# The QKV half-runs of units 1 to 3 moved ahead of the 320-column half-runs of the second product

## The chip, the cores and the metric

The kernel runs on one core of one Trainium2 chip. The metric is the device time of one execution in microseconds (us). Three runs of the kernel before gave 1107.3, 1107.57 and 1108.79 us, with a median of 1107.57 us.

Five engines work side by side and are tied together by semaphores: TensorE (PE in the profile, with its weight loads shown apart as PEld), VectorE (DVE), ScalarE (ACT), GpSimd (POOL), and SyncE (SP), which issues most DMAs. Products are written to PSUM and copied from there to SBUF by ACT or DVE.

## The reference, cut to what matters

```python
xn = _layernorm(x)                                   # 2048 x 576
qkv = xn @ wqkv                                      # 576 x 1728; 32 heads of 18
idx = pos[:, None] - 2 * arange(8)[None, :]          # window 8, dilation 2
logits = where(idx >= 0, (q . k[idx]) * 18 ** -0.5, -1e9)
o = softmax(logits) . v[idx]                         # per head
h = maximum(xn @ w1, 0)                              # 576 x 4608
return x + o @ wo + h @ w2                           # 4608 x 576
```

## The kernel before, in words

**Phases and token blocks.** A window with dilation 2 joins only tokens of one parity, so the kernel runs two phases (`ph` 0 and 1), the even and the odd 1024 tokens. A phase has four token blocks (`tb`) of 256. Products are float32 split into a high and a low part, and the PE array is used as two halves of 64 rows, so matmuls come in pairs.

**Groups and steps.** After some plain products (the slots) the MLP of a phase runs in 30 groups `g` of eight steps each (`group`, `step`). A step has first a block of the first product (w1), six pairs of 256 columns into a PSUM bank of the pools `ph` and `pm`; I call it an **R block**. Then it has one half of a run of the second product (w2), `o_half`, six pairs into a buffer of the pool `po`. A run of the second product is a piece: 256 or 320 columns of the output, two halves. The 320-column pieces have their halves at steps 2 and 3 and at steps 6 and 7, the 256-column pieces at steps 4 and 5 and at steps 8 and 1 of the next group. I call these halves **O320** and **O256**. A finished piece is copied out by ACT (`evict`, L746) and added to the output by a POOL-issued DMA (L752).

**QKV.** The heads are split into four units of eight heads. Unit 0 belongs to the slots and is not touched. Units 1, 2 and 3 start at groups 5, 11 and 17 of each phase. For each token block, `qkv_half` runs a first half of 14 pairs and a second half of 13 pairs of 432 columns (L142 in `mm_rows`), into one buffer of `po`; after the second half ACT copies the result to the attention arena `att` (L533): four copies in an odd unit, where V has rows of its own, two in an even unit. In the units touched, one token block takes half a group, so a unit lasts two groups.

**Pools.** `po` has two buffers of two banks, `pm` and `ph` two each, so that PSUM is full. Second-product pieces and QKV blocks take the two `po` buffers in turn; whoever takes a buffer waits until its last user was copied out.

**Attention.** It runs on DVE, a few operations at a time, from a list `bg` that `run_bg` works off twice per step as far as a count of DVE time against PE time allows (`STEP`, `DUE`, `room`). Per unit the order is: eight multiplications q by k (L575) and eight sums (L578), the last of which is followed by a POOL select for the mask (L581), then the softmax: maximum (L587), subtraction (L590), exponential on ACT (L593), sum (L596), reciprocal (L599), multiplication (L602), then the weighted sum of v (L610, L617) and transposes (L626, L633), and DMAs of the result to the DRAM tile `od` (L639). A unit's attention lasts until the next unit's QKV or beyond: the softmax of unit `u - 1` stands near the first QKV block of unit `u` (that of unit 0 near the first of unit 1).

**What sets the order.** All engines take their instructions in the order in which the program issues them. In `step` that order is: R block, its copies (seeds L1026, kept banks L1030), the eviction of a 256-column piece at even steps, loads and splits that are due (`fire`, weight splits L172, L174, L176), the first `run_bg`, the O half, the eviction of a 320-column piece at odd steps, late copies, `fire` again, then the QKV half that the table `ins` holds for this step (L1272), then the second `run_bg`.

**After unit 3.** With its attention done the output product's weights are loaded (L267, L270) and split (L172 and L176, 576 columns wide), and at the seam between the phases the second phase's transposed tokens `xT` are loaded (L405, L407).

## Time and profile before

| | |
|---|---|
| runs | 1107.3, 1107.57, 1108.79 us; median 1107.57 |
| profiled execution, span | 1106.7 us |
| granted PE clock (slices and windows) | 0.9 or more in each slice; 1.00 in the QKV stretch 164.32 to 209.20 us |
| matmuls and weight loads | 16410 each |
| DVE, ACT, POOL busy | 843.0, 572.3, 358.3 us |
| HBM | 154 GB/s over the span |

The profiled execution's own time is not listed apart from its span; the runs lie 0.6 to 2.1 us above the span, the median 0.9 us above it. A run of the kernel before differs from another by 0.1% (1107.3 against 1108.79).

How to read it: the timeline gives the start and the duration of each instruction, with equal instructions that follow one another merged. Ends of matmuls are modelled, so the pace of PE is read from one start to the next and not from the durations. A row's bracket says how long its engine stood idle before it and which instruction released it. `64*128 64x432` is a matmul with 64 rows of the array, 128 columns of weights and 432 columns of data.

### The profile page before, as it was taken

To read this page: it belongs to the slowest core of one execution; us is meant where nothing else is said; L and a number is where in the kernel's file an instruction comes from. 1 tells how busy PE (TensorE), PEld (TensorE's weight loads), DVE (VectorE), ACT (ScalarE), POOL (GpSimd) and SP (SyncE) were. 2 spreads that over 40 slices of the span, in tenths; PEclk is the share of its full clock that TensorE was granted. 3 is DMA by queue.
4 is the path that set the end of the run, shared out by engine and by line. 5 is a ranking of instruction groups with operands and counts; after the bars stand their busy time and mean duration, and the time that the engine had idled before them with its cause. 6 is when DMAs were issued, how large, how long until landed. Compare 5 with 4: busy or idle time off the path is not lost.

```text
span 1106.7 us, 37929 instructions
## 1 busy us (share of the span) xinstructions
PE 1098.4 (99%) x16410; PEld 1086.7 (98%) x16410; DVE 843.0 (76%) x1262; ACT 572.3 (52%) x1350; POOL 358.3 (32%) x377
## 2 busy tenths in 40 slices
PE   8999999999999999999999999999999999999998
PEld 8999999999999999999999999999999999999998
DVE  7676898898898989994426339987988978989741
ACT  5433563564465366656535246535635644665551
POOL 2313441333333234432211224413423333343321
PEclk9999999999999999999999999999999999999999
DMA  7369995696597598889958258849947965988896
GB/s 236 133 172 218 201 180 98 147 203 108 118 226 133 84 215 159 157 152 251 276 91 174 28 131 166 151 71 191 201 86 157 195 119 117 216 144 168 156 231 144
DMA packets 136598, 177.26 MB, mean 160 GB/s; under 512 B 27872, under 2 KB 83936, under 8 KB 136400
## 3 DMA queue, kind: packets, MB, share of 16 engines
q0 software_dynamic: 37632, 81.40, 47.3%
q1 hardware_dynamic: 98080, 92.55, 28.7%
q8 instruction: 129, 2.11, 0.7%
q10 hardware_dynamic: 720, 0.89, 0.2%
q14 instruction: 37, 0.30, 0.1%
HBM read 74.07 MB, written 96.22 MB: 154 GB/s over the span
## 4 chain that ended last, share of the span: by engine, by line
PE 96%; DMA 1%; DVE 1%; ACT 1%; issue 0%; DVEq 0%; POOL 0%; ACTq 0%
PE po L163 33%; PE po L142 22%; PE ph L163 16%; PE pm L163 13%; PE pm L142 5%; PE ph L142 4%; PE ph L130 1%; PE po L130 1%; DMA xT<-words 1%; PE pm L354 0%; DMA att<-in_x 0%; DVE ar L176 0%; DVE ar L797 0%; ACT ev L746 0%; ACT ar L172 0%
## 5 line engine op out<-in xcount | busy, mean ns | idle before, releaser
L163 PE MATMUL po<-ar 64*128 64x320 f32 (+1 forms) x5760 | 453.1, 290 | 0.6
L163 PEld LDWEIGHTS po<-ar 64*128 64x128 f32 x5760 | 394.6, 185 | 2.8 <-ACT ev L746 0.8
L163 PE MATMUL ph<-xT,ar 64*128 64x256 f32 x2520 | 317.5, 275 | 0.4 <-ACT pm L1026 0.4
L752 POOL DMA_DIRECT2D out<-ev x128 | 152.5, 1191 | 475.8 <-ACT ev L746 359.1
L163 PEld LDWEIGHTS ph<-xT,ar 64*128 64x128 f32 x2520 | 285.4, 185 | 1.4 <-ACT pm L1026 1.2
L163 PE MATMUL pm<-xS,ar 64*128 64x256 f32 x2160 | 257.5, 275 | 0.7 <-ACT u L1030 0.2
L746 ACT ACTIVATE ev<-po 128x512 f32<-128x512 f32 (+1 forms) x266 | 172.1, 652 | 137.0 <-PE po L163 78.8
L163 PEld LDWEIGHTS pm<-xS,ar 64*128 64x128 f32 x2160 | 235.8, 185 | 1.8 <-ACT u L1030 1.0
L176 DVE TENSOR_TENSOR ar<-st,ar 128x256 fp32r<-128x256 f32 (+3 forms) x236 | 141.3, 619 | 72.7 <-ACT ar L172 72.3
L172 ACT ACTIVATE ar<-st 128x256 fp32r<-128x256 f32 (+3 forms) x304 | 146.0, 503 | 3.3 <-DMA st<-in_w 2.3
L142 PE MATMUL po<-wq,xT 64*128 64x432 f32 x1296 | 133.4, 353 | 0.0
L142 PEld LDWEIGHTS po<-wq,xT 64*128 64x128 f32 x1296 | 119.2, 185 | 3.0 <-ACT ev L746 0.2
L174 POOL TENSOR_TENSOR ar<-st,ar 128x256 fp32r<-128x256 f32 (+1 forms) x68 | 75.0, 1105 | 130.9 <-ACT ar L172 128.1
L958 POOL TENSOR_TENSOR st<-st 128x256 f32<-128x256 f32 x120 | 112.8, 945 | 6.0 <-DMA st<-in_w 1.8
L163 PE MATMUL ph<-xS,ar 64*128 64x256 f32 x720 | 102.0, 275 | 0.0
L163 PEld LDWEIGHTS ph<-xS,ar 64*128 64x128 f32 x720 | 94.3, 185 | 0.2
L575 DVE TENSOR_TENSOR pr<-att 128x1152 f32<-128x1152 f32 x64 | 90.8, 1431 | 0.1
L610 DVE TENSOR_TENSOR pr<-att 128x1152 f32<-128x1152 f32 x64 | 88.4, 1397 | 0.4
L578 DVE TENSOR_REDUCE att<-pr 128x64 f32<-128x1152 f32 x64 | 85.5, 1343 | 0.1
L617 DVE TENSOR_TENSOR pr<-pr 128x1152 f32<-128x1152 f32 x64 | 71.6, 1119 | 1.4
L142 PE MATMUL po<-ar 64*128 64x256 f32 (+1 forms) x984 | 72.5, 290 | 0.0
L797 DVE SCALAR_TENSOR_TENSOR ar<-ph,ar 128x256 fp32r<-128x256 f32 x96 | 39.1, 418 | 42.3 <-ACT ar L793 41.9
(120 smaller groups left out, 1370.6 us busy)
## 6 DMA issues: line engine op xcount, KB each, us to landing
out<-ev POOLq DMA_DIRECT2D x128, 576.0 KB, 7.1
st<-in_w SPq DMA_DIRECT2D x72, 288.0 KB, 5.6
st<-in_w SPq DMA_DIRECT2D x63, 256.0 KB, 3.4
att<-att SPq DMA_DIRECT2D x16, 441.0 KB, 4.4
att<-in_wqkv SPq DMA_DIRECT2D x28, 216.0 KB, 6.2
od<-att SPq DMA_DIRECT2D x32, 160.0 KB, 5.9
att<-in_x SPq DMA_DIRECT2D x14, 288.0 KB, 4.0
st<-in_w SPq DMA_DIRECT2D x60, 64.0 KB, 6.1
```

The costliest lines, as they stand in the source:

```text
L142: ins = nc.tensor.matmul(o, l[z], r[z], start=start, stop=stop)
L163: b.ins = nc.tensor.matmul(b.ap, l[part], r[part], start=start, stop=stop, skip_group_check=skip)
L172: nc.scalar.activation(hi, src, AF.Copy)
L174: nc.gpsimd.tensor_tensor(lo, src, f32(hi), op=ALU.subtract)
L176: nc.vector.tensor_tensor(lo, src, f32(hi), op=ALU.subtract)
L575: nc.vector.tensor_tensor(pr[i], q, window(k, i), op=ALU.mult)
L578: nc.vector.tensor_reduce(lg[:, i], pr.pop(i).rearrange(heads, d=Dh), axis=AX.X, op=ALU.add)
L610: nc.vector.tensor_tensor(pr[i].rearrange(heads, d=Dh), e, window(v, i).rearrange(heads, d=Dh), op=ALU.mult)
L617: nc.vector.tensor_tensor(o, z[:, :, 0:n], z[:, :, n : 2 * n], op=ALU.add)
L746: nc.scalar.activation(acc[:, :, cols], z[:, :, 0 : cols.stop - cols.start], AF.Copy)
L752: ADDED[ph, tb] = nc.gpsimd.dma_start(rows_of(ph, tb), acc, accum_op=ALU.add)
L958: nc.gpsimd.tensor_tensor(stg(o), stg(a), stg(b), op=op)
```

## The change

The half-runs of one QKV block stand one step earlier (2 and 3, 6 and 7, not 3 and 4, 7 and 8), and in each of these steps they stand ahead of the second product's half and of everything behind it, directly after the first `run_bg`:

```diff
-                a, i = g + tb // 2, 3 + 4 * (tb % 2)
+                a, i = g + tb // 2, 2 + 4 * (tb % 2)
                 ins[ph, a, i].append((qkv_half, (ph, u, tb, False, True)))
                 ins[ph, a, i + 1].append((qkv_half, (ph, u, tb, True, True)))
...
             run_bg(room(i, True, prev == 0))
+            for f, a in ins.pop((ph, g, i), ()):
+                f(*a)
             og, piece = (g - 2, 2 + i // 2) if i < 4 else (g - 1, (i - 4) // 2)
             if og >= 0:
                 o_half(ph, og, piece, i % 2 == 1)
...
             fire(ph, g, i, "O")
-            for f, a in ins.pop((ph, g, i), ()):
-                f(*a)
             run_bg(room(i, False, prev == 0))
```

The number of instructions of the products stays. What moves is shown at three places.

**PE, group 5 of phase 0, steps 2 to 4**, the first QKV block of unit 1 (first rows: the end of step 2's R block). Before:

```order
L163 MATMUL ph<-xT,ar 128x256
L163 MATMUL po<-ar 128x320 x12
L163 MATMUL pm<-xS,ar 128x256 x12
L163 MATMUL po<-ar 128x320 x12
L142 MATMUL po<-wq,xT 128x432 x28
L163 MATMUL pm<-xT,ar 128x256
L163 MATMUL ph<-xS,ar 128x256
```

And now:

```order
L163 MATMUL ph<-xT,ar 128x256
L142 MATMUL po<-wq,xT 128x432 x28
L163 MATMUL po<-ar 128x320 x12
L163 MATMUL pm<-xS,ar 128x256 x12
L142 MATMUL po<-wq,xT 128x432 x26
L163 MATMUL po<-ar 128x320 x12
L163 MATMUL pm<-xT,ar 128x256
```

Before, an R block and an O256 lay between the two halves of QKV, and the second half stood behind that O256; now it is done before the second O320, which is followed directly by step 4's R block. The `po` buffer that QKV used is taken next by step 4's O256 now, and by step 6's O320 before.

**ACT at the same place**, from the seed of step 2 on. Before:

```order
L1026 ACTIVATE ph<-ph 128x256
L746 ACTIVATE ev<-po 128x2x256
L746 ACTIVATE ev<-po 128x2x320
L172 ACTIVATE ar<-st_2809 128x320
L793 ACTIVATE ar<-pm 128x256
L533 ACTIVATE att<-po 128x2x144
L533 ACTIVATE att<-po 128x144
L533 ACTIVATE att<-po 128x2x144
L533 ACTIVATE att<-po 128x144
L1026 ACTIVATE pm<-ph 128x256
L172 ACTIVATE ar<-st 128x256
L593 ACTIVATE att<-att 128x512
```

And now:

```order
L1026 ACTIVATE ph<-ph 128x256
L746 ACTIVATE ev<-po 128x2x256
L593 ACTIVATE att<-att 128x512
L533 ACTIVATE att<-po 128x2x144
L533 ACTIVATE att<-po 128x144
L533 ACTIVATE att<-po 128x2x144
L533 ACTIVATE att<-po 128x144
L746 ACTIVATE ev<-po 128x2x320
L172 ACTIVATE ar<-st_2809 128x320
L793 ACTIVATE ar<-pm 128x256
L1026 ACTIVATE pm<-ph 128x256
```

The four copies of QKV's result stand ahead of the eviction of the 320-column piece, and the softmax's exponential stands ahead of the copies, behind which it stood.

**SP near the end of phase 0**, from the last DMAs of unit 3's attention result on (L200 loads w1 for the next phase, L267 and L270 load the last of the output product's weights). Before:

```order
L639 DMA od<-att 32x5x256 x4
L200 DMA st<-in_w 128x4x384
L202 DMA st<-in_w 64x384 x2
L267 DMA att<-wo_143 128x576
L270 DMA att<-wo_143 64x1x576 x2
```

And now:

```order
L639 DMA od<-att 32x5x256 x4
L267 DMA att<-wo_143 128x576
L270 DMA att<-wo_143 64x1x576 x2
L200 DMA st<-in_w 128x4x384
L202 DMA st<-in_w 64x384 x2
```

The output product's weights are asked for ahead of w1's.

## The prediction

> **What bounds the kernel.** I read the page first, its busy shares and its chain.
>
> ```profile
> PE 1098.4 (99%) x16410; PEld 1086.7 (98%) x16410; DVE 843.0 (76%) x1262; ACT 572.3 (52%) x1350; POOL 358.3 (32%) x377
> PE 96%; DMA 1%; DVE 1%; ACT 1%; issue 0%; DVEq 0%; POOL 0%; ACTq 0%
> ```
>
> PE is busy 1098.4 of 1106.7 us and carries 96% of the chain, so a microsecond of PE waiting is a microsecond of time, and there are at most 8.3 us of idleness to win back. The change leaves PE's work alone. It can act in three ways: on the waits at the two `po` buffers, on the pace at which PE issues, and on what DVE, ACT and DMAs do later because the order of their work moved. For all three I read the timeline around a QKV block, first PE's at unit 1 of phase 0.
>
> ```profile
> 159.85 0.84 PE L163 MATMUL ph<-xT,ar 64*128 64x256 f32 x12
> 160.53 0.84 PE L163 MATMUL po<-ar 64*128 64x256 f32 x12
> ...
> 161.89 1.04 PE L163 MATMUL po<-ar 64*128 64x320 f32 x12
> 162.76 0.85 PE L163 MATMUL pm<-xS,ar 64*128 64x256 f32 x12
> 163.45 1.03 PE L163 MATMUL po<-ar 64*128 64x320 f32 x12
> 164.32 2.87 PE L142 MATMUL po<-wq,xT 64*128 64x432 f32 x28
> 167.03 0.28 PE L163 MATMUL pm<-xT,ar 64*128 64x256 f32 x1
> ...
> 167.74 0.87 PE L163 MATMUL po<-ar 64*128 64x256 f32 x12
> 168.44 2.68 PE L142 MATMUL po<-wq,xT 64*128 64x432 f32 x26
> 170.96 0.28 PE L163 MATMUL ph<-xS,ar 64*128 64x256 f32 x1
> ```
>
> The reader is to see the starts. A 256-column block ahead of QKV takes 160.53 - 159.85 = 0.68 us; an O320 takes 162.76 - 161.89 = 0.87, the R block behind it 0.69. Past the QKV's first half an O256 takes 168.44 - 167.74 = 0.70. QKV's first half took 2.71 (164.32 to step 4's R block at 167.03) and its second 2.52 (168.44 to 170.96). No row has a bracket: PE doesn't wait here.
>
> **The added wait.** This is the largest term. ACT's and DVE's rows at the same place:
>
> ```profile
> 171.16 1.08 ACT L533 ACTIVATE att<-po 128x288 f32<-128x288 f32 x4 [3.14 <-PE po L142]
> ...
> 172.88 0.63 ACT L593 ACTIVATE att<-att 128x512 f32<-128x512 f32 x1
> ```
>
> ```profile
> 164.47 1.34 DVE L578 TENSOR_REDUCE att<-pr 128x64 f32<-128x1152 f32 x1
> 165.73 0.48 DVE L176 TENSOR_TENSOR ar<-st,ar 128x320 fp32r<-128x320 f32 x1
> 166.13 1.34 DVE L578 TENSOR_REDUCE att<-pr 128x64 f32<-128x1152 f32 x1
> 168.57 1.14 DVE L587 TENSOR_REDUCE m<-att 128x64 f32<-128x512 f32 x1 [1.10 <-POOL att L581]
> ...
> 172.09 0.69 DVE L590 TENSOR_TENSOR att<-att,m 128x512 f32<-128x512 f32 x1 [2.05 <-ACT att L533]
> ```
>
> ```profile
> 167.55 0.98 POOL L581 TENSOR_SCALAR_AFFINE_SELECT att<-att 1x448 f32<-1x448 f32 x1 [0.82 <-DVE att L578]
> ```
>
> After the change step 4's O256 takes the `po` buffer that QKV filled, so it waits for the four copies L533 (1.08 us). Let T be the end of step 2's R block, 161.89. PE then runs QKV 2.71, O320 0.87, R 0.69, QKV 2.52, so the copies could start at T + 6.8, or T + 7.0 with the about 0.2 that lie between the last start of QKV and the copies (170.96 to 171.16). Behind QKV stand O320 and R, and O256 is ready at T + 6.79 + 0.87 + 0.70 = T + 8.36. Copies that start at once end at T + 8.1: hidden, with 0.25 us to spare. This holds where nothing stands ahead of them in ACT's queue, so I take nothing for the other 18 of the 24 QKV blocks.
>
> At each unit's first block the exponential L593 now stands ahead of the copies. It needs a chain: sum L578, select L581, maximum, subtraction. In unit 1 of phase 0 both sums still lie ahead. The second now follows the first at 165.73, as L176 moves behind, and ends at 167.07; L581 (0.08 later, 0.98 long) to 168.13; L587 to 169.3; L590 to 169.95; the exponential (0.10 and 0.63) to 170.65; the copies to 171.7. O256 is ready at 161.89 + 8.36 = 170.25: a wait of **1.45 us**. The 320-column eviction waits behind the copies too; its buffer is needed only by the QKV half of step 6, two microseconds later.
>
> Unit 3 has only one sum left there, but its copies also come behind the sum L596 in the order of the writes to `att`.
>
> ```profile
> 345.08 1.04 PE L163 MATMUL po<-ar 64*128 64x320 f32 x12
> ...
> 347.60 2.98 PE L142 MATMUL po<-wq,xT 64*128 64x432 f32 x28
> 350.42 0.28 PE L163 MATMUL pm<-xT,ar 64*128 64x256 f32 x1
> ```
>
> ```profile
> 346.95 0.60 ACT L746 ACTIVATE ev<-po 128x512 f32<-128x512 f32 x1 [1.26 <-DMA out<-ev]
> ```
>
> ```profile
> 347.67 1.34 DVE L578 TENSOR_REDUCE att<-pr 128x64 f32<-128x1152 f32 x1
> ...
> 356.93 1.18 DVE L596 TENSOR_REDUCE r<-att 128x64 f32<-128x512 f32 x1 [0.25 <-ACT att L593]
> ```
>
> ```profile
> 890.45 1.04 PE L163 MATMUL po<-ar 64*128 64x320 f32 x12
> ```
>
> ```profile
> 892.48 1.34 DVE L578 TENSOR_REDUCE att<-pr 128x64 f32<-128x1152 f32 x1
> ```
>
> By the same durations, from the start of the last L578: 1.34 + 0.08 + 0.98 + 0.04 + 1.14 + 0.65 + 0.73 + 1.20 (L596) + 1.08 = 7.24 to the end of the copies. In phase 1 this is 892.48 + 7.24 = 899.72 against 890.45 + 8.36 = 898.81: **0.9 us**. In phase 0 it is 354.91 against 353.44, 1.5 us; the DVE rows ahead of it can run earlier by half a microsecond as POOL's mixing (L958) moves away, so I take **1.0**. Unit 2 has one sum left, and its two copies need not follow L596: if that sum starts as late after T as unit 3's (2.6 us in phase 0, 2.0 in phase 1), they end at T + 8.5 and T + 7.9, the first less half a microsecond as in unit 3, which is just hidden. In unit 1 of phase 1 the exponential was done well ahead of the copies before already:
>
> ```profile
> 710.24 0.63 ACT L593 ACTIVATE att<-att 128x512 f32<-128x512 f32 x1 [2.11 <-DVE att L590]
> ```
>
> The sum is 1.45 + 1.0 + 0.9 = **3.3 us**. Below: 1.5, if unit 3's copies don't follow L596 (and nothing if DVE runs a microsecond and a half earlier than I read). Above: 6, if the three first blocks that I count as hidden wait about as long as unit 3's, 0.9 each.
>
> The Trainium skill ("TensorE: Matmul & The Clock Gate", section "Architectural detail: the array is 16× 32×32, not 1× 128×128") says that ScalarE and VectorE take their queues strictly in order and that only TensorE pulls weight loads ahead. By it the copies can't pass the exponential, which speaks against this change. The trace agrees in the other direction: DVE's L590 stood idle for 2.05 us until ACT's copies were done.
>
> **The removed wait.** In unit 3 of phase 0 the QKV's first half was held by the eviction at 346.95, itself late because a DMA had not freed its `ev` buffer. It took 350.42 - 347.60 = 2.82 us in place of 2.71, and began 2.52 us after T (345.08 to 347.60) in place of 2.43 (161.89 to 164.32). Now QKV takes the older buffer, and the O320 that needs the late one stands behind 2.7 us of QKV: **-0.2 us**. Nothing is late next there. Its bounds are 0 and -0.3.
>
> **The pace.** Where it comes back:
>
> ```profile
> 208.32 1.04 PE L163 MATMUL po<-ar 64*128 64x320 f32 x12
> 209.20 0.28 PE L163 MATMUL pm<-xT,ar 64*128 64x256 f32 x1
> ...
> 209.89 0.84 PE L163 MATMUL po<-ar 64*128 64x256 f32 x12
> 210.57 0.27 PE L163 MATMUL ph<-xS,ar 64*128 64x256 f32 x1
> ```
>
> ```profile
> 173.08 1.04 PE L163 MATMUL po<-ar 64*128 64x320 f32 x12
> ...
> 174.66 1.04 PE L163 MATMUL po<-ar 64*128 64x320 f32 x12
> ```
>
> From the first QKV on, 164.32, 256-column blocks take 0.70 in place of 0.68 us (as at 167.74), until an R block that directly follows a second O320, at 209.20; the block from 209.89 to 210.57 has 0.68 again. In the groups with QKV the second O320 was always followed by QKV (as the one at 174.66), so the slow pace lasted 45 us in each unit. The first O320 didn't bring it back: with the R block behind it, it took 174.66 - 173.08 = 1.58 us, against 163.45 - 161.89 = 1.56 ahead of QKV. After the change each second O320 is directly followed by an R block. If the pace came back there, five blocks of each half-group would have it until the next QKV (R, O256, R, O256, R): 5 times about 0.024, or 0.12 us, in each of 24 half-groups, -2.9 us. The other end is 0, or a tenth of a us on the wrong side, since the slow stretch begins one step earlier. The row at 209.20 speaks for the gain, but there no QKV stood just ahead of the O320, as it will now; the row at 173.08 speaks against it. Between them I take the middle, **-1.4 us**, and keep both ends.
>
> The Trainium skill ("TensorE: Matmul & The Clock Gate", section "Back-to-back issue gap") gives the isolated gap of matmuls as columns over 2.4 plus 2.5 ns, a thing of the columns alone; six pairs of 256 columns would take an estimated 0.66 us wherever they stand, and the sum would have no pacing term. The 0.68 and 0.70 above disagree about the "wherever".
>
> **Later effects.** PE lost some time behind the softmax in a group without QKV:
>
> ```profile
> 445.91 0.28 PE L163 MATMUL pm<-xT,ar 64*128 64x256 f32 x1
> 446.33 0.97 PE L163 MATMUL po<-ar 64*128 64x256 f32 x12
> ```
>
> The last gap is 446.33 - 445.91 = 0.42 where 0.11 is usual (six in 0.68); the maximum and subtraction move ahead there, so I take **-0.3** (0 to -0.3). At the seam PE waits for tokens and ACT:
>
> ```profile
> 509.05 10.54 DMA xT<-words
> ```
>
> ```profile
> 515.97 0.68 ACT L172 ACTIVATE wq<-att 128x576 fp32r<-128x576 f32 x1
> ```
>
> ```profile
> 517.57 0.38 PE L163 MATMUL pm<-xS,ar 64*128 64x256 f32 x1 [0.18 <-ACT u L1030]
> ```
>
> After the change unit 3's attention ends half a group earlier in the order, and the wide splits of the output product's weights leave this crowded stretch. The one at 515.97 cost ACT 0.68 ahead of the copy L1030 that PE waited for. I take this one, **-0.7**; the bounds are +0.7 (one waits in ACT for its load) and -2 (three such splits).
>
> **The sum.** 3.3 - 0.2 - 1.4 - 0.3 - 0.7 = +0.7 us on the profiled execution, span 1106.7, so 1107.4. The median of the runs lies 0.9 above that span: 1107.57 + 0.7 = **1108.3 us**. A measurement of this kernel can tell about 0.2%, 2.2 us, from no change: 1105.35 to 1109.8.
>
> **Rivals.**
> - *The pace comes back at every second O320*, and the waits are as forecast: -2.9 for -1.4 gives 1106.8; chance 0.15. For it speaks 209.20, against it 173.08.
> - *The pace follows the columns alone or doesn't come back behind QKV*: 0 for -1.4 gives 1109.7; chance 0.15. For it speaks that a QKV half stands right ahead of each O320 now. By the gap formula of the Trainium skill ("TensorE: Matmul & The Clock Gate", section "Back-to-back issue gap") this is the case.
> - *Slower: the exponential blocks the copies in all six first blocks.* The point is T + 7.0: where DVE brings the exponential's input 0.7 us ahead of that or later, PE pays. Unit 2 is just at this point, and one more multiplication or split ahead of L587 in DVE is enough. Price 0.9 to 1.0 in each of three more blocks, +2.9: 1111.2; chance 0.19. For it speaks the little slack; against it, that unit 1 of phase 1 had its exponential at 710.24, well ahead.
> - *No wait at all*, because DVE, freed of waits such as the 2.05 us above, runs ahead and the copies start at once: 0 for 3.3 gives 1105.0; chance 0.09. Against it: the chain behind L578 has no idle time in it to lose.
>
> **How the numbers follow.** The forecast has the remaining 0.42. Faster than 1105.35 are the no-wait case in six of ten (0.05), a sixth of the first rival with a better seam, and small parts of the forecast: together 0.15. Slower than 1109.8 are most of the slower rival (0.17), nearly half of the second (0.07) and a little of the forecast (0.04): 0.28. The range reaches from 1104.2, below the no-wait case, to 1111.8, above the slower one with half a microsecond more at the seam.
>
> **What would show it.** The timeline of PE has a gap of 1 to 1.5 us ahead of step 4's O256 at the first QKV block of unit 1 (phase 0) and of unit 3 (both phases), released by ACT's L533, with L593 directly ahead of it on ACT, and none at the other blocks. The R block behind each second O320 shows 0.68 (pace back) or 0.70. The gap ahead of 347.60 is gone. If the copies start 3 us after L590 everywhere, or O256 waits at tb 1 to 3 as well, the added wait was too small; if PE's gaps at the seam grow, the later effects have the wrong sign.

## The result and the profile after

| | before | after |
|---|---|---|
| median of six runs, us | 1108.70 (1107.30 to 1112.00) | 1116.12 (1115.31 to 1118.34) |
| profiled execution, span, us | 1106.7 | 1114.1 |
| ratio, 95% interval | | 1.0069 (1.0058 to 1.0079) |

The changed kernel is slower by 0.7%. On the median of 1107.57 us of the prediction this is 1115.2 us, outside its range of 1104.2 to 1111.8.

The page of the changed kernel, busy times and chain:

```profile
PE 1101.5 (99%) x16410; PEld 1087.0 (98%) x16410; DVE 856.5 (77%) x1262; ACT 570.5 (51%) x1350; POOL 359.1 (32%) x377
PE 88%; ACT 3%; DVE 3%; issue 3%; DMA 2%; POOL 1%; POOLq 0%; DVEq 0%; ACTq 0%
```

PE has the same 16410 matmuls, but its share of the chain fell from 96% to 88%: ACT, DVE and POOL now stand in the chain that sets the end. What PE waits for, from the view of its waits (total us, times, longest):

```profile
PE po L163 <- ACT att L533: 2.1, 3, 0.9
...
PE ph L163 <- issue: 1.3, 2, 1.1
PE po L163 <- ACT ev L746: 0.9, 3, 0.6
PE ph L163 <- ACT pm L1026: 0.9, 4, 0.2
```

Of these four rows the same view of before has only the last, with 0.4 us in 2 waits. The first is the wait that the prediction added. The second and third are new.

This view counts idle time only, and a wait also delays the next matmuls by about 0.1 us. The table below therefore goes by blocks. For each block of PE it takes the distance from its start to the next block's start, less the usual one (0.695 us for 256 columns, 0.88 for 320, 2.715 and 2.524 for QKV's halves), and books what is over to the instruction that PE waited for. "Pace" is the sum of the small remainders, as a difference to before. The program was profiled a second time (*again*).

| us | copies L533 | evictions L746 | seeds L1026, L1030 | no releaser | seam, 514 to 560 | start of phase 1 | pace | span |
|---|---|---|---|---|---|---|---|---|
| before | 0 | 0.8 | 1.6 | 0 | 2.5 | 1.6 | 0 | 1106.7 |
| after | 3.0 | 1.8 | 3.2 | 2.0 | 1.4 | 2.2 | +0.4 | 1114.1 |
| again | 2.0 | 3.0 | 2.7 | 0.6 | 1.5 | 2.2 | +0.8 | 1113.1 |

The differences of the second row to the first add up to 7.5 us against 7.4 in the spans, those of the third to 6.3 against 6.4. The copies take 2 to 3 us. The rest is spread: evictions and seeds together 2.6 to 3.3, the start of phase 1 0.6, pace 0.4 to 0.8, waits without a releaser 0.6 to 2.0, less 1.1 at the seam.

The place of the prediction, unit 1 of phase 0, in the timeline of the changed kernel. PE:

```profile
161.99 2.88 PE L142 MATMUL po<-wq,xT 64*128 64x432 f32 x28
164.72 1.04 PE L163 MATMUL po<-ar 64*128 64x320 f32 x12
166.30 2.68 PE L142 MATMUL po<-wq,xT 64*128 64x432 f32 x26
168.82 1.04 PE L163 MATMUL po<-ar 64*128 64x320 f32 x12
170.83 0.97 PE L163 MATMUL po<-ar 64*128 64x256 f32 x12 [0.27 <-ACT att L533]
```

ACT:

```profile
169.04 0.63 ACT L593 ACTIVATE att<-att 128x512 f32<-128x512 f32 x1 [5.94 <-DVE att L590]
169.70 1.08 ACT L533 ACTIVATE att<-po 128x288 f32<-128x288 f32 x4
170.64 0.74 ACT L746 ACTIVATE ev<-po 128x640 f32<-128x640 f32 x1
171.22 0.50 ACT L172 ACTIVATE ar<-st 128x320 fp32r<-128x320 f32 x1
...
174.30 0.37 ACT L1026 ACTIVATE pm<-ph 128x256 f32<-128x256 f32 x1 [2.30 <-DVE ar L797]
...
175.72 0.61 ACT L746 ACTIVATE ev<-po 128x512 f32<-128x512 f32 x1
```

DVE:

```profile
168.25 0.69 DVE L590 TENSOR_TENSOR att<-att,m 128x512 f32<-128x512 f32 x1
171.76 0.49 DVE L176 TENSOR_TENSOR ar<-st,ar 128x320 fp32r<-128x320 f32 x1 [2.81 <-ACT ar L172]
172.17 1.17 DVE L596 TENSOR_REDUCE r<-att 128x64 f32<-128x512 f32 x1
173.38 0.55 DVE L599 RECIPROCAL r<-r 128x64 f32<-128x64 f32 x1
173.85 0.36 DVE L797 SCALAR_TENSOR_TENSOR ar<-pm,ar 128x256 fp32r<-128x256 f32 x1
```

The copies L533 stand behind the exponential L593 as forecast, and PE waits for them at 170.83. A second effect is one that the prediction did not follow. The second O320 starts at 168.82, 5.4 us later than at 163.45 before, because both halves of QKV now stand ahead of it (2.71 + 2.52). All that may start only when it is done is late too: the eviction L746 of the 320-column piece (170.64, before 164.52), and with it the split of that step's weights, L172 on ACT and L176 on DVE (before at 165.73). DVE takes its instructions in order, so it stands idle for 2.81 us ahead of L176, and what is queued behind runs late, L797 last. In the timeline of the kernel before, this L797 had no wait. Its row, and those of the two evictions on ACT:

```profile
169.63 0.41 DVE L797 SCALAR_TENSOR_TENSOR ar<-pm,ar 128x256 fp32r<-128x256 f32 x1
```

```profile
164.52 0.71 ACT L746 ACTIVATE ev<-po 128x640 f32<-128x640 f32 x1 [1.53 <-PE po L163]
...
174.25 0.60 ACT L746 ACTIVATE ev<-po 128x512 f32<-128x512 f32 x1
```

L797 is 4.2 us later, at 173.85. The seed L1026 waits for it, and behind the seed in ACT's queue stands the eviction of the 256-column piece, 175.72 in place of 174.25. The next O320 needs its buffer. In unit 1 of phase 0 it comes just in time; in unit 1 of phase 1 PE pays. The same links there, on ACT and then on PE:

```profile
723.83 0.37 ACT L1026 ACTIVATE pm<-ph 128x256 f32<-128x256 f32 x1 [3.30 <-DVE ar L797]
...
725.26 0.60 ACT L746 ACTIVATE ev<-po 128x512 f32<-128x512 f32 x1
```

```profile
725.91 1.15 PE L163 MATMUL po<-ar 64*128 64x320 f32 x12 [0.59 <-ACT ev L746]
```

I call this the **queue chain**: late O320, eviction and split, DVE's queue, L797, seed, next eviction, next O320.

### The profile page after: what moved, and what is told of

It is laid out like the page before. It is cut to its first block, busy times and chain, and to the rows that moved or that the text cites. A ratio compares the mean times of both kernels' runs of the same rounds, so it can differ in the third digit from the quotient of the medians.

```text
span 1114.1 us, 37928 instructions
## 1 busy us (share of the span) xinstructions
PE 1101.5 (99%) x16410; PEld 1087.0 (98%) x16410; DVE 856.5 (77%) x1262; ACT 570.5 (51%) x1350; POOL 359.1 (32%) x377
## 4 chain that ended last, share of the span: by engine, by line
PE 88%; ACT 3%; DVE 3%; issue 3%; DMA 2%; POOL 1%; POOLq 0%; DVEq 0%; ACTq 0%
PE po L163 30%; PE po L142 20%; PE ph L163 15%; PE pm L163 11%; PE pm L142 5%; PE ph L142 4%; PE ph L130 1%; PE po L130 1%; DMA out<-ev 1%; ACT ev L746 1%; DMA st<-in_w 1%; ACT ar L172 1%; POOL st L958 1%; DVE ar L176 1%; DVE ar L797 0%
## 5 line engine op out<-in xcount | busy, mean ns | idle before, releaser
L163 PE MATMUL po<-ar 64*128 64x320 f32 (+1 forms) x5760 | 459.6, 290 | 3.4 <-ACT att L533 2.1
L163 PEld LDWEIGHTS po<-ar 64*128 64x128 f32 x5760 | 403.4, 184 | 7.6 <-ACT ev L746 2.8
L752 POOL DMA_DIRECT2D out<-ev x128 | 153.3, 1198 | 519.6 <-ACT ev L746 265.5
L746 ACT ACTIVATE ev<-po 128x512 f32<-128x512 f32 (+1 forms) x266 | 172.9, 654 | 122.5 <-PE po L163 57.0
L176 DVE TENSOR_TENSOR ar<-st,ar 128x256 fp32r<-128x256 f32 (+3 forms) x236 | 147.5, 645 | 75.4 <-ACT ar L172 75.1
L172 ACT ACTIVATE ar<-st 128x256 fp32r<-128x256 f32 (+3 forms) x304 | 146.6, 504 | 19.4 <-PE pm L163 15.3
L958 POOL TENSOR_TENSOR st<-st 128x256 f32<-128x256 f32 x120 | 117.6, 985 | 9.5 <-DMA st<-in_w 5.4
L797 DVE SCALAR_TENSOR_TENSOR ar<-ph,ar 128x256 fp32r<-128x256 f32 x96 | 39.0, 418 | 39.6 <-ACT ar L793 39.4
```

The costliest lines, as they stand in the source:

```text
L163: b.ins = nc.tensor.matmul(b.ap, l[part], r[part], start=start, stop=stop, skip_group_check=skip)
L172: nc.scalar.activation(hi, src, AF.Copy)
L176: nc.vector.tensor_tensor(lo, src, f32(hi), op=ALU.subtract)
L746: nc.scalar.activation(acc[:, :, cols], z[:, :, 0 : cols.stop - cols.start], AF.Copy)
L752: ADDED[ph, tb] = nc.gpsimd.dma_start(rows_of(ph, tb), acc, accum_op=ALU.add)
L958: nc.gpsimd.tensor_tensor(stg(o), stg(a), stg(b), op=op)
```

## The experiments

Ratios are to the kernel before, run beside it on the same chip, with a 95% interval; times are medians. In a unit, PE may wait at two places: I call the O256 of step 4, behind the unit's first QKV block, the **first place**, and the O320 of step 6, behind the first half of its second QKV block, the **second place**.

**again**: the changed kernel once more, no edit.

> The changed kernel once more. Its first profile lost 7.2 us of PE time in waits that the kernel before did not have: 3.0 at the first QKV blocks of three units, where step 4's O256 waited for QKV's copies; about 1.8 at the second blocks of three units, where an O320 waited for the eviction of a 256-column piece; about 1.2 at seeds; and 1.8 in two gaps (318.4 and 327.6 us) that nothing releases, put down to issue. Theory A (late ACT and DVE queues) expects the waits of the first two kinds again at the same places, within 0.1 us. If the issue gaps belong to the program they stand at the same places again, with the span near 1114; if they are chance they are gone or elsewhere, with a span near 1112.

Measured: 1116.88 us, 1.0056 (1.0036 to 1.0076). The waits for copies in units 1 and 3 of phase 0 are there again, and so are those at the second place (0.3, 0.9 and 0.2 us in unit 3 of phase 0 and units 1 and 3 of phase 1); the wait for copies in unit 3 of phase 1 and the two waits without a releaser are not. A wait of 1 us can come and go between executions; the two spans differ by 1.0 us.

### Does the exponential cost it?

**exp_behind**: the exponential is held back until QKV's copies are issued.

```diff
-        while bg and t["dve"] ...
+        while bg and not (bg[0][1].__name__ == "sm_exp" and keep_exp) and t["dve"] ...
...
+            if ins.get((ph, g, i)) and ins.get((ph, g, i + 1)):
+                keep_exp.add(0)
             run_bg(room(i, True, prev == 0))
...
+            if i % 4 == 3:
+                keep_exp.clear()
             run_bg(room(i, False, prev == 0))
```

> The changed kernel, with the softmax's exponential of the unit before held back until the first QKV block's second half and its copies are issued. Theory A (the copies stand behind the exponential in ACT's queue, and the 320-column weight split behind the copies holds DVE's queue): the waits of 0.55, 1.26 and 1.22 us ahead of step 4's O256 go, the split L172 comes about a microsecond earlier and with it DVE, so the two waits of 0.43 at the second block of unit 3 go as well; the one of 0.98 in unit 1 of phase 1 stays. 3 to 4 us less than the changed kernel, about 1112.5. Rival B (the time is lost to PE's own issue and pace, or to the attention's changed order as a whole): within 1 us of the changed kernel.

Measured: 1122.21 us, 1.0098 (1.0073 to 1.0123), where I had expected 1112.5. The copies' waits went from 3.0 to 0.4 us, and the evictions' rose from 1.8 to 8.0. DVE and then PE in unit 1 of phase 1:

```profile
724.21 2.63 DVE L610 TENSOR_TENSOR pr<-att 128x1152 f32<-128x1152 f32 x2
726.76 0.42 DVE L797 SCALAR_TENSOR_TENSOR ar<-pm,ar 128x256 fp32r<-128x256 f32 x1
```

```profile
729.35 1.97 PE L163 MATMUL po<-ar 64*128 64x320 f32 x12 [3.17 <-ACT ev L746]
```

The softmax that waits for the exponential stands ahead of L797 in DVE's queue, and here its lateness reaches the second place.

**exp_after_l797**: the same, but held until step 4's L793 and L797 are issued, so that the softmax stands behind them.

```diff
+            elif i % 4 == 0:
+                keep_exp.clear()
             run_bg(room(i, True, prev == 0))
```

> The changed kernel, with the exponential (and with it all softmax work behind it) held back until the copies L793 and L797 of step 4 are issued, one run of the attention list later than in the kernel that held it behind the copies of QKV only. Theory A2: DVE brings L797 as soon as ACT's L793 is there, the seed and the eviction are in time, and the copies are not held: the waits at the first and second blocks of all units go, 3 to 5 us under the changed kernel, 1112 to 1113.5; the attention that is pushed back may cost some of it at later seeds. If holding the exponential is bad in itself, as the kernel that held it one step less (1122.2) could be read: at 1120 or above.

Measured: 1117.38 us, 1.0075 (1.0062 to 1.0088). Waits for seeds fell to 0.3 us, and none is left at the second place. The copies' waits stay (2.7 us) although the exponential is behind them, since the copies write the arena that the subtraction L590 is still working on, as ACT's row shows:

```profile
169.00 1.08 ACT L533 ACTIVATE att<-po 128x288 f32<-128x288 f32 x4 [6.45 <-DVE att L590]
```

What was won went at the end of the kernel, where the attention, later now, held the output product: from its first matmul to the end of the span the kernel takes 37.7 us in place of 32.4, 5.3 more.

**softmax_held_u3**: from the maximum on held until L797, in unit 3 only.

```diff
-        while bg and t["dve"] ...
+        while bg and not (bg[0][1].__name__ == "sm_max" and keep_max) and t["dve"] ...
...
+            if g >= 17 and ins.get((ph, g, i)) and ins.get((ph, g, i + 1)):
+                keep_max.add(0)
+            elif i % 4 == 0:
+                keep_max.clear()
             run_bg(room(i, True, prev == 0))
```

> The changed kernel, with the softmax of unit 2's attention (from the maximum L587 on) held back at unit 3's first QKV block, in both phases, until step 4's L793 and L797 are issued; units 1 and 2 as in the changed kernel. Theory A3 (the copies L533 wait for whatever softmax operation on the arena att was issued ahead of them, on DVE as well as on ACT, and the second block's O320 waits because L797 stands behind the same softmax): unit 3 has no wait ahead of step 4's O256 (0.9 to 1.2 us before) and none at the second block's O320 (0.3 to 0.5), in both phases, while unit 1 of phase 0 keeps 0.4 to 1.0 and unit 1 of phase 1 its 0.9 at the second block. 2.5 to 3 us of waits less near 355 and 905 us; what the later end of the attention costs at the seam and at the end of the kernel is open, so 1112.5 to 1117 in time. Rival (the copies wait for ACT's queue alone): the wait ahead of step 4's O256 in unit 3 is unchanged from the kernel that held only the exponential, 1.1 us.

Measured: 1136.03 us, 1.0226 (1.0198 to 1.0254), 19 us beyond what I had expected at most. In unit 3 of both phases no wait is left at the first and second places, neither for copies nor for evictions: the softmax operations issued ahead are what the copies wait for. Its price is elsewhere: the attention of unit 3 ends later, which costs 12.5 us at the seam (before: 2.5), and from the output product's first matmul to the end of the span it takes 45.6 us (before: 32.4). Part of this is the clock: behind the waits there it was granted at 0.50 in two windows of 6.83 us (from 527.95 and 545.02) and two of 3.41 us (from 1104.81 and 1125.29).

### Does the late split cost it?

**split_late**: the split of the 320-column weights at a unit's first block is issued one step later, behind L793 and L797.

```diff
-                on(ph, a + 1, 3, "O", w2_split, ph, f + 1, (1,))
+                on(ph, a + 1, *((4, "T") if a + 1 in (5, 11, 17) else (3, "O")), w2_split, ph, f + 1, (1,))
```

> The changed kernel, with the split of the 320 weight columns that stands at step 3 of groups 5, 11 and 17 (L172 on ACT, L176 on DVE) moved behind the copies L793 and L797 of step 4. Theory A: DVE no longer waits for this split ahead of L797, so the seed of step 5 and the eviction of step 6 come in time and the waits of 0.43, 0.98 and 0.43 at the second blocks go; the waits for the copies at the first blocks stay. About 1.8 us less, 1114.3. Rival (the second blocks wait because the first blocks ran late, whatever the split): no more than 0.5 us less.

Measured: 1115.98 us, 1.0055 (1.0031 to 1.0080). The waits at the second place in unit 3 and in unit 1 of phase 1 are gone, but 0.7 us is new in unit 2 of phase 0 and the seam takes 3.3 us in place of 1.5 (again). The total is that of *again*, 1.0056.

**exp_and_split**: both edits.

> Both edits, the exponential behind the copies and the 320-column split behind L793 and L797. Theory A: waits at the first and the second blocks go, 4.5 to 5 us less than the changed kernel, about 1111.4; what is left against the kernel before is the seeds' 1.2, the issue gaps if they stay, and a pace that is not better. Rival B: within 1 us of the changed kernel. A third theory (the added waits only move to the next taker of a buffer) expects the two edits to give less together than the larger of them alone plus half a microsecond.

Measured: 1126.13 us, 1.0136 (1.0112 to 1.0160), where I had expected 1111.4. At the second place PE waits 1.6 to 4.4 us in five of the six units, and 0.5 us in unit 1 of phase 0.

In all of these kernels the attention's operations stand elsewhere than in the kernel before, so that more than one thing differs. The next kernels fix this.

### The queue chain, link by link

**old_attention_order**: the changed kernel, with the number of attention operations at each of the 976 calls of `run_bg` fixed to that of the kernel before. DVE's order is then that of before row for row, and on ACT only the copies stand elsewhere.

```diff
-        while bg and t["dve"] + bg[0][0] / 960.0 <= t["pe"] + margin and not (ran and bg[0][0] == 0):
+        for _ in range(int(next(calls))):
```

> The changed kernel, with the attention list worked off exactly as in the kernel before: as many operations at each of the 976 places as there. DVE's order is then that of the kernel before, row for row, and ACT's differs only by the copies L533, which stand ahead of the 320-column eviction and the exponential behind them. Theory A4 (the change does harm in two ways: the planner's counts put softmax ahead of the copies, and the 320-column split L172 and L176, which may start only behind the second O320, now comes 5.2 us of QKV later, while DVE, in order, holds the last sum L578, L587 and L797 behind it): the waits for the copies go, as no softmax stands ahead of them; at the second block of units 1 to 3 the O320 (or the seed ahead of it) waits longer, 1 to 2.5 us each where the sum stands behind the split: about as slow as the changed kernel, 1113 to 1117. Rival (the planner's changed order is the whole cause): within 2 us of the kernel before, 1108 to 1111.

Measured: 1122.03 us, 1.0122 (1.0104 to 1.0140). So the loss does not need the planner's shifted order, a rival theory: with the old order the change costs more. No wait for copies is left; at the second place of units 1 to 3 of phase 0 PE waits about 2.2 us each. DVE, then PE:

```profile
170.80 0.49 DVE L176 TENSOR_TENSOR ar<-st,ar 128x320 fp32r<-128x320 f32 x1 [5.17 <-ACT ar L172]
171.21 1.35 DVE L578 TENSOR_REDUCE att<-pr 128x64 f32<-128x1152 f32 x1
173.66 1.15 DVE L587 TENSOR_REDUCE m<-att 128x64 f32<-128x512 f32 x1 [1.10 <-POOL att L581]
174.72 0.41 DVE L797 SCALAR_TENSOR_TENSOR ar<-pm,ar 128x256 fp32r<-128x256 f32 x1
```

```profile
177.87 1.15 PE L163 MATMUL po<-ar 64*128 64x320 f32 x12 [2.04 <-ACT ev L746]
```

Here the chain stands alone: DVE idles 5.17 us for the late split (the QKV halves that moved ahead of the O320 take 5.23), and behind it the sum, the select, the maximum and L797 follow one another. The waits are not all that this profile shows: behind each of the three, the clock was granted at 0.50 for 3.41 us, and QKV's next half-run took 1.0 to 1.4 us longer than its usual 2.52. This execution was the slowest of the five (1126.24 us); another, with a mean granted clock of 1.00, took 1121.60.

**old_order_split_late**: the same with the edit of *split_late*.

> The same, with the 320-column split of groups 5, 11 and 17 moved behind L793 and L797 of step 4. Theory A4: both harms are gone, no waits over 0.3 us at first and second blocks; what is left is the pace (0.4 to 0.8) and a seed now and then: 1108.5 to 1111.5, 4 us or more under the kernel with the old attention order alone. Rival (the cushion that QKV's second half gave between L797 and the seed is lost whatever stands ahead of L797): waits of 0.5 us or more stay at the second blocks, and the time stays at 1112 or above.

Measured: 1116.75 us, 1.0072 (1.0058 to 1.0086), on the same chip 5.3 us less than *old_attention_order*, though not the 1108.5 to 1111.5 that I had expected. The waits at the second place in phase 0 fell to 1.4 to 1.5 us and didn't go; beside them the two profiles differ by smaller waits in phase 1 and by the clock, which is at 1.00 behind these waits now. **old_order_split_again** is the same kernel beside the next one:

> The kernel of old_order_split_late once more, beside old_order_select_first on one chip: 1.0072 of the kernel before within the interval 1.0058 to 1.0086 of its first run, waits of 1.3 to 1.5 us at the second QKV block of units 1 to 3 of phase 0.

Measured: 1116.38 us, 1.0054 (1.0041 to 1.0066). Its POOL, DVE and PE:

```profile
170.79 1.20 POOL L752 DMA_DIRECT2D out<-ev  x1 [6.63 <-ACT ar L793]
171.56 0.99 POOL L581 TENSOR_SCALAR_AFFINE_SELECT att<-att 1x448 f32<-1x448 f32 x1
```

```profile
172.58 1.18 DVE L587 TENSOR_REDUCE m<-att 128x64 f32<-128x512 f32 x1 [5.62 <-POOL att L581]
173.69 0.41 DVE L797 SCALAR_TENSOR_TENSOR ar<-pm,ar 128x256 fp32r<-128x256 f32 x1
```

```profile
177.24 1.15 PE L163 MATMUL po<-ar 64*128 64x320 f32 x12 [1.33 <-ACT ev L746]
```

The second link is POOL's queue. The DMA L752 that adds the late eviction to the output waits 6.63 us for it, and the mask select L581, long ready, stands behind. The page names L793 as the releaser; the DMA reads `ev`, which the eviction L746 just ahead of L793 wrote.

**old_order_select_first**: in addition the DMA L752 is issued behind the select at these blocks. Nothing else moves on any engine, and on POOL only in three places.

```diff
-            ADDED[ph, tb] = nc.gpsimd.dma_start(rows_of(ph, tb), acc, accum_op=ALU.add)
+            (kept.append if wait_add else lambda f: f())(lambda: ADDED.__setitem__((ph, tb), nc.gpsimd.dma_start(rows_of(ph, tb), acc, accum_op=ALU.add)))
...
-            run_bg(room(i, True, prev == 0))
+            run_bg(room(i, True, prev == 0)); i == 3 and g in (5, 11, 17) and wait_add.add(0); i == 4 and [wait_add.clear(), [kept.pop()() for _ in range(len(kept))]]
```

> The kernel of old_order_split_late, with one thing more: at the first QKV block of units 1 to 3 of phase 0, POOL issues the DMA of the late 320-column eviction (L752) behind the mask select (L581) and not ahead of it. Nothing else moves on any engine. Theory (POOL's queue is the next link of the chain): L581 runs as soon as the last sum L578 is done, at about 166.2, L587 ends by 168.4 and no longer holds L797, which then starts when L793 is done, at about 170.6 in place of 173.51; the seed follows at about 171.1 in place of 174.02, and the eviction of the 256-column piece ends by 174, ahead of the 175.6 at which O320 is ready. The waits at the second QKV block of the three units (1.4 to 1.5 us each) are gone: 4.2 to 4.5 us less than old_order_split_late, 1112 to 1113 us. Rival (POOL's queue is only beside the path; the cushion of QKV between L797 and the seed is what is missing): the waits of 1 us and more at 177, 269 and 363 stay and the time is within 1 us of old_order_split_late.

Measured: 1111.78 us, 1.0022 (1.0011 to 1.0033), 4.6 us less than its base on the same chip. POOL, DVE and PE:

```profile
166.32 0.99 POOL L581 TENSOR_SCALAR_AFFINE_SELECT att<-att 1x448 f32<-1x448 f32 x1 [2.00 <-DVE att L578]
170.75 1.20 POOL L752 DMA_DIRECT2D out<-ev  x1 [3.45 <-ACT ar L793]
```

```profile
170.89 0.41 DVE L797 SCALAR_TENSOR_TENSOR ar<-pm,ar 128x256 fp32r<-128x256 f32 x1
```

```profile
175.70 1.04 PE L163 MATMUL po<-ar 64*128 64x320 f32 x12
```

L797 is 2.8 us earlier, and the O320 starts right behind QKV with no bracket. No wait is left at any QKV block. *old_attention_order* was slower than the kernel before by 13.5 us (1.22% of 1108.99). By medians the two links in order-bound queues made 5.3 and 4.6 of them. By the ratios, each to the kernel before on its own chip, they made 0.50% and 0.32%, or 5.5 and 3.6 us; the kernel between them had 1.0072 on one chip and 1.0054 on the other. For POOL's link the profiles agree with the larger figure: the spans are 1114.5 and 1109.9 us. The 0.2% that remain are spread, among them two waits of 0.3 us for evictions and one of 0.6 without a releaser, and were not taken apart.

### Step and place apart

**place_only**: QKV ahead of the O half, in its old steps. **steps_only**: QKV in its new steps, behind the O half.

```diff
# place_only, against the changed kernel
-                a, i = g + tb // 2, 2 + 4 * (tb % 2)
+                a, i = g + tb // 2, 3 + 4 * (tb % 2)
# steps_only, against the kernel before
-                a, i = g + tb // 2, 3 + 4 * (tb % 2)
+                a, i = g + tb // 2, 2 + 4 * (tb % 2)
```

> Half of the change: the QKV half-runs stay at steps 3, 4, 7 and 8 but stand ahead of the second product's halves. Theory A2 (what was lost is the cushion: before, QKV's second half stood between step 4's copies L793 and L797 and the seed of step 5, and gave DVE 2.5 us more to bring L797; with it, DVE's softmax work ahead of L797 was free; the changed kernel has only an O256 and an R block there): the cushion is kept, since QKV's second half stands behind step 4's R block, so no waits at the second blocks and none at the copies, where the exponential stands behind them again: within 2 us of the kernel before, 1107.5 to 1110. Rival A (placing QKV ahead of the halves changes who takes which buffer, and that is what costs): 3 us or more over the kernel before.

> The other half of the change: the QKV half-runs move to steps 2, 3, 6 and 7 but stay behind the second product's halves. Theory A2: the cushion is gone here too, as QKV's second half ends before step 4's R block; the copies have more time (an R, O256, R, O256 and R until the next taker), so the 3 us of the first blocks go, but the waits of DVE's L797 and ACT's seeds stay in some form: 2 to 5 us over the kernel before, 1111 to 1114. Rival A (the buffer order and the copies are all that costs): the kernel before within 1 us, 1108 to 1110.

Measured: place_only 1112.88 us, 1.0036 (1.0022 to 1.0049); steps_only 1124.10 us, 1.0137 (1.0123 to 1.0151), 10 us beyond what I had expected at most. Neither part alone is free. The waits of *steps_only*:

```profile
PE po L142 <- ACT ev L746: 7.8, 14, 1.4
```

Its QKV needs a buffer whose eviction comes late at nearly every block. In *place_only* QKV's first half waits 0.5 to 0.9 us for evictions at five places and the O320 0.5 us for copies at two, while the pace comes back by 2.0 us. Two more kernels take its waits apart.

**place_old_order**: *place_only* with the attention's order of before, so that only PE's order differs from the kernel before. **place_chain_cut**: in addition the two links cut as in *old_order_select_first*.

> The kernel of place_only (QKV's halves in their old steps 3, 4, 7, 8, but ahead of the second product's half) with the number of attention operations at each call fixed to that of the kernel before, so that DVE, ACT, POOL and SP have the order of before row for row and only PE's order differs. If the queue chain is the cause (the 320-column eviction, now 2.7 us later, holds L172, L176, the sum, POOL's select and the maximum, and these L797): L797 of the first block of a unit in phase 0 starts near 172 in place of 169.6, the eviction of the 256-column piece ends near 175.5, and QKV's first half at about 174.6 waits 0.5 to 1 us there in units 1 to 3; no waits of the O halves on copies; the pace comes back by about 2 us as in place_only; together 0.999 to 1.002 of the kernel before. If the waits of place_only came from the planner's shifted order: no waits at all, 0.997 to 0.999.

> The kernel of place_old_order with the two links cut as in old_order_select_first: the 320-column weight split of the first QKV block of a unit one step later (behind L793 and L797), and in phase 0 POOL's DMA issue of that eviction behind the mask select. Theory of the queue chain: no wait at any QKV block, the pace comes back by about 2 us, nothing else changes: 0.997 to 0.999 of the kernel before, faster by some 1 to 3 us. Rival (the cushion is missing or the pace doesn't come back with this order): waits at QKV's first half of step 7, 1.000 or more.

Measured: 1112.51 us, 1.0031 (1.0019 to 1.0042), and 1108.14 us, 0.9994 (0.9985 to 1.0003). Cutting the links takes 4.4 us and nearly all waits: evictions 5.8 to 0.9 us, copies 1.2 to 0. So the chain explains *place_only* too. What is left is the time of the kernel before within its uncertainty, not a gain: the pace is 1.7 us better in the profile, whose span is 1106.0.

### The pace, and parts of the change

**second_half_first**: the kernel before, with QKV's second half alone ahead of the O256 in steps 4 and 8.

```diff
             run_bg(room(i, True, prev == 0))
+            for f, a in ins.pop((ph, g, i), ()) if i % 4 == 0 else ():
+                f(*a)
```

> The kernel before, with one thing changed: QKV's second half stands ahead of step 4's and step 8's O256, not behind it; steps and the first half stay. Only PE's order differs, in 24 places; ACT's, DVE's and POOL's orders are the same. Theory on the pace (in the kernel that moved only the place, each O256 directly behind QKV's second half took 0.68 us and all blocks behind it as well; behind QKV followed by an R block or an O320 the slow 0.70 stayed): the pace comes back in each half-group, 5 or 6 blocks of 0.025 us each, 2 to 3 us in all: about 1106 where the kernel before has 1108.8. Buffers: O256's is evicted 5 us ahead, the copies have 2.8 us, so no new wait. Rival (the pace there came back by the waits that stood near, or follows the columns alone): no change within 0.7 us.

Measured: 1109.26 us, 0.9994 (0.9980 to 1.0008). No new wait and no gain: behind QKV's second half the 256-column blocks keep 0.70 us. The theory that the pace returns where an O256 directly follows QKV's second half falls. In the changed kernel (first fence) the blocks stand at 0.70 as well; in *place_chain_cut* (second) the pace is back:

```profile
182.18 0.87 PE L163 MATMUL po<-ar 64*128 64x256 f32 x12
182.88 0.87 PE L163 MATMUL ph<-xT,ar 64*128 64x256 f32 x12
183.59 0.87 PE L163 MATMUL po<-ar 64*128 64x256 f32 x12
```

```profile
170.36 0.87 PE L163 MATMUL po<-ar 64*128 64x256 f32 x12
171.75 0.84 PE L163 MATMUL po<-ar 64*128 64x256 f32 x12
173.11 1.04 PE L163 MATMUL po<-ar 64*128 64x320 f32 x12
```

From 171.75 an O256 and an R block take 1.36 us, two of 0.68. What brings the pace back stays open.

**later_blocks_only** and **first_blocks_only**: the change for the 18 blocks behind the first of each unit alone, and for the 6 first blocks alone.

```diff
# TEST is tb == 0 for later_blocks_only, tb > 0 for first_blocks_only
-                a, i = g + tb // 2, 2 + 4 * (tb % 2)
+                a, i, ins = g + tb // 2, 2 + 4 * (tb % 2), ahead
+                if TEST:
+                    i, ins = i + 1, behind
```

> The change for the second to fourth QKV block of each unit only (18 of 24 blocks); the first blocks stay as in the kernel before. Theory A3 (nearly all of the loss comes from the softmax of the unit before, which stands beside the first block and which the copies, the 320-column split and L797 meet in ACT's and DVE's queues): no wait for L533 and none at the second block's O320; what is left is the pace (0.5 us), small waits at seeds, and a changed attention order: 1 to 3 us over the kernel before. Rival (a cost of 0.3 us at each moved block, for the shorter cushion): 18 of 24 of the whole loss, 5 us or more over the kernel before.

> The change for the first QKV block of each unit only (6 of 24 blocks); the others stay as in the kernel before. Theory A3: the waits ahead of step 4's O256 (2 to 3 us in sum) are there in unit 1 of phase 0 and in unit 3, and step 5's seed is late as in the changed kernel; the second block's QKV, behind the O320s again, meets the late eviction there: 3 to 5.5 us over the kernel before. Rival (0.3 us at each moved block): 6 of 24 of the loss, under 2 us over the kernel before.

Measured: 1115.27 us, 1.0052 (1.0034 to 1.0071), and 1116.87 us, 1.0059 (1.0047 to 1.0071). Each costs nearly the whole, so the parts don't add. With the first blocks alone it is in the seeds (5.7 us, before 1.6). With the later ones it lies in many small waits, among them 1.0 without a releaser and one of 1.1 for an eviction in a group without QKV, and 1.1 more at the seam. In *old_order_select_first* the same 18 blocks stand moved too, and PE waits at none of them; so this loss seems to come with the planner's shifted choices. By which links was not taken apart.

## Why the prediction was wrong

**The added wait** (forecast 3.3 us) was right in its places and nearly in size: 3.0 us in this profile, 2.0 in the second. By place it was 1.45, 1.0 and 0.9 forecast against 0.4, 1.15 and 1.1 (and 0.1 for the restart of each), so the sum came nearer than its parts, by luck. Nor is the exponential in ACT's queue the whole mechanism: with it behind the copies, in *exp_after_l797*, 2.7 us of such waits stayed, for softmax operations on DVE.

**The step that failed** is the sentence beside it: "The 320-column eviction waits behind the copies too; its buffer is needed only by the QKV half of step 6, two microseconds later." About that buffer it was right: the eviction ends at 171.38, and the QKV half of step 6 starts at 173.77 without a wait. But it asked only who needs the buffer, and not what stands behind the eviction and its split in the queues of DVE and POOL. The runs show in its place the queue chain: cutting its DVE link gave 5.3 us (with a part for the clock) and its POOL link 3.6 to 4.6 in the order of before, and both together 4.4 with QKV in the old steps. In the changed kernel itself the planner had moved the softmax ahead. There 1.8 us are waits at the second places; evictions and seeds as a whole are up by 2.6 to 3.3, of which 0.5 lie at 494 in a group without QKV, and why the start of phase 1 takes 0.6 more is not shown. That cutting the links recovers just these in the planner's own order is not shown: *split_late* cut one, and the time went elsewhere.

A second step failed beside it: "I take nothing for the other 18 of the 24 QKV blocks." Moved alone, with the planner's own choices, they cost 0.5% (*later_blocks_only*); by which links stays open.

**The removed wait** (-0.2) was right in the first profile, where the 0.17 us at 347 are gone; in the second the O320 behind QKV waits 0.14 us for the same eviction.

**The pace** (-1.4) had the wrong sign: +0.4 and +0.8. The rival "doesn't come back behind QKV" was right, and by its own price would have added 1.4. That rival took the gap formula of the Trainium skill ("TensorE: Matmul & The Clock Gate", section "Back-to-back issue gap") along. The formula is stated there for an isolated matmul. In this program 256-column blocks have 0.68 and 0.70 us, so one gap for one width doesn't describe it.

**Later effects**: the seam gave 1.1 us (forecast 0.7). The stall at 445 (-0.3) only moved to 447, with 0.5 us left, and another of 0.5 came at 494.

**The slower rival** had the right sign by the wrong link: the exponential holds the copies in three blocks as forecast, not six, and *exp_behind* showed that holding it behind the copies makes the kernel slower.

**Not foreseen** were waits without a releaser, 2.0 us in one profile and 0.6 in the other. The sum by terms of the first: 3.0 + 1.0 + 1.6 + 2.0 - 1.1 + 0.6 + 0.4 = 7.5, where 3.3 - 0.2 - 1.4 - 0.3 - 0.7 stood.

## What to carry to other kernels

When a block is put ahead of another on the bounding engine, list everything that may start only after the one put back (eviction, buffer release, weight split, DMA issue), and for each what is queued behind it on its in-order engine: a wait of 5 us that harms nobody where it stands can hold an unrelated instruction that the bounding engine needs. A work item that looks movable may be the cushion that hides such a chain, and removing one link first uncovers the next, here DVE's and then POOL's. Try a schedule change with the planner's choices frozen to the old ones as well; only then does a difference belong to the moved blocks alone.

## What the hardware showed unexpectedly

**The clock after a wait.** In *old_attention_order* the O320 at 177.87 had waited 2.04 us. The window behind it (columns: window, length, busy times of PE, PEld, DVE, ACT, POOL, granted clock, DMA share, GB/s):

```profile
178.00:183.00 5.00, 5.00 (x44) 4.79 (x46) 4.93 (x8) 0.33 (x1) 0.00 (x0) 0.66 0.00 0
```

The granted clock is 0.66 there, and 0.50 from 179.38 on for 3.41 us, so a wait of 2 us can cost more than itself. After the wait of 1.34 us in *old_order_split_late* it stayed 1.00 at the same place. But it also stayed 1.00 after one of 2.06 us in *exp_after_l797* (the output product's matmul at 1101.68), so the length of the wait alone doesn't decide it. The Trainium skill ("TensorE: Matmul & The Clock Gate", section "What's actually happening") puts the gate's step down behind an idle window of about 3.4 us. Here it came behind 2.04 us of waiting.

**Waits without a releaser.** In three of the nineteen profiles PE stood still in one and the same block, here in the changed kernel:

```profile
319.53 0.27 PE L163 MATMUL ph<-xT,ar 64*128 64x256 f32 x1 [1.12 <-issue]
```

It lies beside SP's load of the next unit's QKV weights (316.41 in that trace); *later_blocks_only* has it ahead of 319.31 (0.85 us) and *old_order_select_first* ahead of 318.41 (0.59), the second profile of the changed kernel doesn't. Its cause stays open.

**POOL in order.** A DMA issue that waits for its data holds a ready select behind it (6.63 us at L752). This agrees with the strict order for GpSimd that the Trainium skill states ("TensorE: Matmul & The Clock Gate", section "Architectural detail: the array is 16× 32×32, not 1× 128×128").
